# An attention and ReGLU kernel in static order: other planning figures, and 160 groups of exponentials on VectorE in place of 158

## The chip, the core and the metric

The kernel runs on one core of a Trainium2 chip. The core has five engines that each work through a queue of their own in order: TensorE (PE in the profile; PEld is its loading of weights), VectorE (DVE), ScalarE (ACT), GpSimd (POOL) and SyncE (SP), which here issues nearly all DMAs. The metric is the device time of one execution in microseconds. Several executions of one build are taken and their median is compared. Besides these, one execution is recorded by the hardware profiler; all durations below come from it.

## The reference

The input x has 2048 rows of 512. After a layer norm, two branches are added to x: attention with 32 heads of 16, and a feed-forward part with 1792 hidden units.

```
xn = layernorm(x)
q, k, v = split(xn @ wqkv)                       # 32 heads of 16
p = softmax(q k^T / 4);  A = (p v) @ wo
g = xn @ W_gate;  h = relu(g) * (xn @ W_up);  B = h @ W_down
out = x + A + B
```

Heads are so narrow that the softmax is the large part: 32 x 2048 x 2048 exponentials, 134 million.

## The kernel before

**Tiles and blocks.** The queries are cut into four chunks of 512 (c4), the heads into four groups of eight (gg), and each group is passed over twice (ee), four heads at a time. That makes 32 blocks. A block goes over 16 key tiles of 128 keys. One key tile of a block holds scores for 4 heads x 128 keys x 512 queries, that is four PSUM banks of 128 x 512.

**Two ways to take the exponential.** Usually a key tile becomes two *units* of two banks each. For a unit, TensorE writes the two banks of scores (L1461 loads k), ScalarE takes the exp of both in one instruction (L1525, 128 x 1024) into a ring of SBUF buffers, and TensorE multiplies them with v (L1433 loads v) into an accumulating bank. The score banks of ScalarE are two pairs; the next but one unit reuses a pair, so a score waits for the exp two units earlier.

For some key tiles, called *groups* here (`quad` in the code, `QUADS` by block), VectorE makes the exponential out of integers: it evicts each of the four score banks with an addition and a maximum into 16-bit integers that, read as bf16, are a stepwise power of two (L1481). GpSimd then makes two copies shifted by a constant, 64 bits at a time (`int64_add`, L1495); for the first two and the last two groups VectorE does that (L1498). All three versions are multiplied with v and add up, which smooths the steps. So a group costs four evictions, two additions and three passes with v, where a key tile on ScalarE costs two exps and one pass. Before, 158 of 512 key tiles are groups: 708 exps and 632 evictions. Where in its block a group stands follows from `QUADS` and `QOFF`; block 0 has none.

**Work beside attention.** The projections of q and k (`proj_q`, `proj_k`), the feed-forward part (`glu`, in pairs of 128 hidden units with two weight buffers, evictions L1130 and L1134) and the rows of the output (`out_rows`, L1172 and L1178, which multiply with W_down in Wd, Wk and Wv and with wo in Wo_p) are called *jobs*. They get places counted in units: projections some 32 to 48 units ahead of their use, feed-forward and rows spread evenly up to `NU - 60`, where NU is the number of units. Weights of the feed-forward part are fetched `W_LEAD` units before their job, in four pieces 6 units apart; rows of an output block come at the earliest `ROW_AT` units after the block of queries ends.

**What sets the order.** Nothing is decided on the chip. `Graph.run` simulates the engines with a fixed duration for each operation (`dur`), a hand-over time for each engine (`LAT`) and priorities, and so lists every engine's instructions; `Graph.emit` writes these lists out with the semaphore waits that they need. An exp counts 904 ns and a hand-over of 176, a GpSimd addition 1060 and 150, an eviction 601 and 135. A group's scores may be made up to `AHEAD` = 10 units before its own place. Filler matmuls are let in ahead of a score only if the plan says that the score is still in time for ScalarE (`fits`). What runs on the chip is the list, each instruction starting when its engine is free and its waits are over.

## Time and profile before

| | before |
|---|---|
| median of 3 runs | 684.08 us (683.42 to 684.76) |
| the profiled execution's own time | 682.77 us |
| its span, first to last instruction | 680.6 us |
| granted TensorE clock | 1.000 of full speed |
| first and last start of an exp | 10.3 and 668.4 us |
| DMA traffic | 28.77 MB, 42 GB/s on average |

The span is shorter than the time by the 2.17 us around it. In the groups of instructions, a row gives the line, engine, operation, the tiles written and read, the number of instructions, then the busy time in us and the mean duration of one in ns, then the idle time of the engine just ahead of them and who ended it. Instructions of one engine overlap (an exp's record is 1117 ns long while the next one starts after some 900), so a duration isn't a step. Matmul ends are modelled. The table of 20 us stretches gives, for each engine, busy us and the number of instructions.

### The profile page before, as it was taken

The numbers are of one execution on the slowest core, as the hardware profiler recorded it, in microseconds if no ns is written. First come the engines' busy times: TensorE is split into PE (matmuls) and PEld (weight loads), VectorE is DVE, ScalarE is ACT, GpSimd is POOL, SyncE is SP. The second block draws the span as 40 slices with busy tenths as digits, with TensorE's granted clock in tenths as the row PEclk, the third lists the DMA queues.
The fourth block names the chain that finished last, engine by engine and source line by source line (L and its number), as shares of the span: only waits on it lengthen the run. The fifth ranks groups of instructions, "written<-read, shape, count | busy, mean of one in ns | idle before, by whom it ended". The sixth has DMA issues, their size and how long they took to land.

```text
span 680.6 us, 46065 instructions
## 1 busy us (share of the span) xinstructions
PE 671.9 (99%) x22322; PEld 397.0 (58%) x20890; DVE 587.0 (86%) x993; ACT 659.8 (97%) x725; POOL 330.8 (49%) x341
## 2 busy tenths in 40 slices
PE   8999999999999999999999999999999999999997
PEld 3565665557565556566655656655555665655574
DVE  8957997999999878888999886889999887998876
ACT  7999999999999999999999999999999999999984
POOL 3302443564556555544556654445556654546540
PEclk9999999999999999999999999999999999999999
DMA  6520011133200121010101111110100121120001
GB/s 202 88 51 21 19 38 42 46 90 80 69 21 21 37 57 44 21 37 16 41 10 23 42 46 50 26 40 22 35 5 21 36 78 33 43 60 13 21 13 35
DMA packets 51478, 28.77 MB, mean 42 GB/s; under 512 B 18840, under 2 KB 50328, under 8 KB 51288
## 3 DMA queue, kind: packets, MB, share of 16 engines
q1 hardware_dynamic: 51144, 25.70, 14.8%
q8 instruction: 169, 2.77, 1.7%
q14 instruction: 21, 0.17, 0.1%
q10 hardware_dynamic: 144, 0.13, 0.1%
HBM read 18.22 MB, written 2.10 MB: 30 GB/s over the span
## 4 chain that ended last, share of the span: by engine, by line
PE 85%; ACT 10%; DVE 4%; issue 0%; DMA 0%; POOL 0%; DVEq 0%
PE ps L138 85%; ACT ring L1525 10%; DVE stats L810 1%; DMA x_sb<-in_A_x_dram 0%; DVE qd L1481 0%; DVE xn_sb L833 0%; DVE qd L1498 0%; DVE mv L812 0%; DVE xn_sb L1298 0%; POOL rstd L794 0%; DVE v_aug L978 0%; DVE kT L971 0%; DVE xnT L878 0%; DVE qT L1065 0%; DVE up_sb L1277 0%
## 5 line engine op out<-in xcount | busy, mean ns | idle before, releaser
L1525 ACT ACTIVATE ring<-ps 128x1024 bf16<-128x1024 f32 x708 | 651.9, 1117 | 7.3 <-PE ps L138 6.5
L1495 POOL INT64_ADD qd<-qd x308 | 317.3, 1040 | 308.9 <-DVE qd L1481 173.5
L138 PE MATMUL ps<-qT,kT 64*32 64x512 bf16 x8192 | 464.5, 375 | 1.2 <-DVE kT L971 0.4
L1481 DVE TENSOR_SCALAR qd<-ps 128x512 int16<-128x512 f32 x632 | 412.8, 684 | 59.6 <-PE ps L138 53.0
L138 PE MATMUL ps<-qd,v_aug 64*32 64x512 bf16 x3792 | 302.2, 375 | 0.2
L138 PE MATMUL ps<-ring,v_aug 64*32 64x512 bf16 x2832 | 242.4, 375 | 0.1
L1461 PEld LDWEIGHTS <-kT 64*32 64x32 bf16 x8132 | 175.3, 92 | 110.0 <-issue 24.4
L1433 PEld LDWEIGHTS <-v_aug 64*32 64x32 bf16 x5252 | 128.6, 92 | 63.9 <-issue 10.1
L138 PE MATMUL ps<-xnT,wgs 64*32 64x512 bf16 x1792 | 137.0, 375 | 0.0
L138 PE MATMUL ps<-xnT,wus 64*32 64x512 bf16 x1792 | 135.3, 375 | 0.0
L138 PE MATMUL ps<-Wd,hT 64*32 64x512 bf16 x768 | 58.6, 375 | 0.3 <-issue 0.2
L913 PEld LDWEIGHTS <-hT 64*32 64x32 bf16 x1792 | 43.9, 92 | 24.1 <-issue 3.7
L913 PEld LDWEIGHTS <-wgs 64*32 64x32 bf16 x1792 | 43.7, 92 | 22.8 <-issue 3.5
L913 PEld LDWEIGHTS <-wus 64*32 64x32 bf16 x1792 | 43.8, 92 | 22.5 <-issue 3.3
L1130 DVE COPY up_sb<-ps 128x512 f32<-128x512 f32 x56 | 38.3, 685 | 7.3 <-PE ps L138 7.3
L138 PE MATMUL ps<-Wv,hT 64*32 64x512 bf16 x512 | 40.3, 375 | 0.4 <-issue 0.4
L1134 DVE SCALAR_TENSOR_TENSOR hT<-ps,up_sb 128x512 bf16<-128x512 f32 x56 | 38.3, 683 | 2.7 <-PE ps L138 2.5
L138 PE MATMUL ps<-Wk,hT 64*32 64x512 bf16 x512 | 39.6, 375 | 0.0
L138 PE MATMUL ps<-Wo_p,x_sb 64*32 64x512 bf16 x480 | 37.7, 376 | 0.1
L138 PE MATMUL ps<-xnT,Wq 64*32 64x512 bf16 x480 | 37.1, 375 | 0.0
L138 PE MATMUL ps<-xnT,Wk 64*32 64x512 bf16 x480 | 35.9, 375 | 0.3 <-DVE xnT L878 0.3
L138 PE MATMUL ps<-Wv,xnT 64*32 64x512 bf16 x512 | 30.4, 375 | 0.3
(83 smaller groups left out, 222.3 us busy)
## 6 DMA issues: line engine op xcount, KB each, us to landing
wus<-in_B_W_up_dram SPq DMA_DIRECT2D x38, 128.0 KB, 2.4
wgs<-in_B_W_gate_dram SPq DMA_DIRECT2D x38, 128.0 KB, 2.5
xr_sb<-in_A_x_dram SPq DMA_DIRECT2D x16, 128.0 KB, 2.7
qT<-qf SPq DMA_DIRECT2D x120, 16.0 KB, 2.3
o_sb<-o_sb SPq DMA_DIRECT2D x60, 32.0 KB, 2.6
out_dram<-xn_sb SPq DMA_DIRECT2D x15, 128.0 KB, 1.9
x_sb<-in_A_x_dram SPq DMA_DIRECT2D x8, 128.0 KB, 2.7
Wd<-in_B_W_down_dram SPq DMA_DIRECT2D x6, 128.0 KB, 2.7
```

What stands on the lines that cost most here:

```text
L138: return e.add_instruction(mybir.InstMatmult(name=e.bass.get_next_instruction_name(), engine=mybir.EngineType.PE, ins=[e.lower_ap(x), e.lo ...
L810: G.op("DVE", 580, lambda e, m=m: e.bn_stats(stats[:, m, :], xs(m)), reads=[t_xm[m]], writes=[t_st], prio=pr, order=last_xn if m == 4 and ...
L913: e.ldweights(w()[rows, 32 * j:32 * j + 32], tile_position=(rows.start, 32 * j))
L1130: G.op("DVE", 603, lambda e: e.tensor_copy(up_sb[:, tup.slot, :], bank_of(tu)), reads=[tu], writes=[tup], prio=-590)
L1134: G.op("DVE", 603, lambda e: e.scalar_tensor_tensor(out=hT[:, th.slot, :], in0=bank_of(tg), scalar=0.0, in1=up_sb[:, tup.slot, :], op0=ALU ...
L1433: e.ldweights(vs(j), tile_position=(64 * half, 32 * j))
L1461: e.ldweights(ks(m), tile_position=(64 * half, 32 * m))
L1481: G.op("DVE", 601, lambda e, j=j, tx=tx: e.tensor_scalar(qd[:, tq.slot, 512 * j:512 * j + 512], ps[:, BANK[tx.slot], :], IBIAS[3], 0.0, op ...
L1495: G.op("POOL", POOL_NS, lambda e, x=x, n=n: e.int64_add(x().bitcast(I64), raw().bitcast(I64), SHIFTS[n + 1] * LANES), reads=[ti, tq, t_lib ...
L1525: exp_ops[u] = G.op("ACT", 904, lambda e, tr=tr, k0=k0: e.activation(ring[:, tr.slot, :, :], ps[:, 4 * k0:4 * k0 + 2, :], ACTF.Exp, scale= ...
```

## The change

Constants change, the planner gets faster bookkeeping, and one line of its rules is new. In the plan an exp now counts 917 ns with a hand-over of 158, a GpSimd addition 1014 ns, and a GpSimd instruction that depends on TensorE, ScalarE or VectorE can start only 110 ns later than before. The groups are 160, at other places: `QUADS` says how many by block, `QOFF` where in the block, and `QUAD_SHIFT` moves single groups by one key tile. `JOB_SHIFT` moves single jobs by some units. Feed-forward and rows are spread to `NU - 68`. The weights of the feed-forward part are fetched 34 units ahead, those of W_down 3.5 units apart, and rows come at the earliest 22 units after a chunk. The maps `release` and `known` and the counter `left` remember what was searched anew each time.

```
-D_STEP = 3
-W_LEAD = 38
+D_STEP = 3.5
+W_LEAD = 34
-ROW_AT = 20
+ROW_AT = 22
-QOFF = 0.3
+QOFF = 0.2
-JOB_SHIFT = {}
-QUAD_SHIFT = {}
+JOB_SHIFT = {2: -1, 6: -4, 9: 3, 13: 4, 14: -1, 33: -1, 34: -4, 36: 2, 41: -2, 47: 1, 49: 4, 50: 1, 51: -4, 53: -1, 59: -9, 71: 2, 72: -4, 73: -1, 75: -2, 78: -2, 79: 3, 80: -1, 83: 5, 84: -4, 88: -1, 89: -1, 92: -1, 97: 4}
+QUAD_SHIFT = {(1, 3): 1, (2, 1): -1, (4, 0): -1, (6, 0): 1, (6, 3): 1, (7, 0): 1, (7, 2): 1, (8, 1): 1, (8, 4): 1, (8, 5): 1, (9, 0): 1, (9, 3): -1, (13, 1): -1, (16, 0): -1, (16, 3): 1, (18, 4): -1, (20, 2): 1, (23, 0): -1, (25, 4): -1, (26, 2): -1, (28, 0): 1, (28, 3): -1, (29, 3): 1, (30, 0): -1, (31, 1): 1}
-POOL_NS = 1060
+POOL_NS = 1014
+PACE_END = 68
+ACT_NS = 917
-QUADS = [0, 3, 4, 5, 5, 6, 5, 5, 5, 5, 6, 5, 5, 5, 5, 6, 5, 5, 5, 6, 5, 5, 5, 5, 6, 5, 5, 5, 5, 6, 5, 5]
+QUADS = [0, 2, 5, 5, 6, 6, 4, 5, 6, 5, 5, 5, 6, 5, 5, 8, 5, 5, 4, 6, 6, 4, 6, 5, 5, 5, 5, 5, 5, 6, 5, 5]
...
-    LAT = {"PE": 212.0, "ACT": 176.0, "DVE": 135.0, "POOL": 150.0, "SP": 0.0}
+    LAT = {"PE": 212.0, "ACT": 158.0, "DVE": 135.0, "POOL": 150.0, "SP": 0.0}
     SWITCH = 107.0
+    TO_POOL = 110.0
...
-                at = max(at, d.end - (self.OWN if d.eng == o.eng == "DVE" else 0.0) if ...
+                at = max(at, (self.TO_POOL if o.eng == "POOL" and d.eng not in ("POOL", "SP") else 0.0) + d.end - (self.OWN if d.eng == o.eng == "DVE" else 0.0) if ...
...
-            at += n * max((NU - 60 - at) / max(rest, 1), 1.0)
+            at += n * max((NU - PACE_END - at) / max(rest, 1), 1.0)
...
-            exp_ops[u] = G.op("ACT", 904, lambda e, tr=tr, k0=k0: e.activation(...
+            exp_ops[u] = G.op("ACT", ACT_NS, lambda e, tr=tr, k0=k0: e.activation(...
```

More of the change, by code (lines that the diff above doesn't have):

```diff
@@ L127, in __init__ @@
         self.r = []
+        self.left = 0
 class Op:
@@ L132 @@
                  "done", "left", "users", "signal", "sem", "val", "waits", "stream", "lat", "seq", "cseq", "hb", "after", "mode", "half", "bank", "urgent", "slack", "port",
-                 "load", "wsrc", "wkey", "wwaits", "pair")
+                 "load", "wsrc", "wkey", "wwaits", "pair", "held")
 def matmul_loaded(e, out, w, x, start, stop, at):
@@ L215, in run @@
             o.users = []
+            o.held = []
+        for t in {t for o in ops for t in o.acq} | {c for o in ops for t in o.acq for c in t.pool.cur if c is not None}:
+            us = set(t.w + t.r)
+            t.left = len(us)
+            for o in us:
+                o.held.append(t)
         for o in ops:
@@ L238, in slot_for @@
                 else:
-                    us = c.w + c.r
-                    if not all(u.done for u in us):
-                        continue
-                    at = max(u.end for u in us)
+                    at = release.get(c)
+                    if at is None:
+                        if c.left:
+                            continue
+                        at = release[c] = max(u.end for u in c.w + c.r)
                 if best is None or at < best[0]:
@@ L261, in run, with bound, ready @@
         last = {}
-        def ready(o):
+        known, release = {}, {}
+        def bound(o):
             at = 0.0
             for d in o.deps:
-                at = max(at, d.end - (self.OWN if d.eng == o.eng == "DVE" else 0.0) if d.eng == "PE" or d.eng == o.eng == "DVE" else d.end + ((0.0 if d.urgent else max(self.DMA_SLACK, o.slack)) if d.eng == "SP" else o.slack))
+                at = max(at, (self.TO_POOL if o.eng == "POOL" and d.eng not in ("POOL", "SP") else 0.0) + d.end - (self.OWN if d.eng == o.eng == "DVE" else 0.0) if d.eng == "PE" or d.eng == o.eng == "DVE" else d.end + ((0.0 if d.urgent else max(self.DMA_SLACK, o.slack)) if d.eng == "SP" else o.slack))
             for d in o.order:
                 at = max(at, d.start if d.eng == o.eng else d.end)
+            return at
+        def ready(o):
+            at = known.get(o)
+            if at is None:
+                at = known[o] = bound(o)
             for t in o.acq:
@@ L403, in run @@
             o.done = True
+            for t in o.held:
+                t.left -= 1
             o.seq = len(self.queue[e])
@@ L426, in run @@
                 pe["mode"] = o.mode
-                pe["at"] = at if o.mode != "half" else min(at, max(pe["at"] + self.ISSUE, ready(o), behind.end if behind is not None else 0.0))
+                pe["at"] = at if o.mode != "half" else min(at, max(pe["at"] + self.ISSUE, bound(o), behind.end if behind is not None else 0.0))
             else:
@@ L1524, in bass_parallel_sum__mha_block__glu_gated_reglu__prompt_kernel @@
             tr = Tile("r%d" % u, P_ring)
-            exp_ops[u] = G.op("ACT", 904, lambda e, tr=tr, k0=k0: e.activation(ring[:, tr.slot, :, :], ps[:, 4 * k0:4 * k0 + 2, :], ACTF.Exp, scale=EXP_SCALE),
+            exp_ops[u] = G.op("ACT", ACT_NS, lambda e, tr=tr, k0=k0: e.activation(ring[:, tr.slot, :, :], ps[:, 4 * k0:4 * k0 + 2, :], ACTF.Exp, scale=EXP_SCALE),
                               reads=[ts], writes=[tr], prio=u - 100, order=[exp_ops[u - 1]] if u else [], name="ex%d" % u)
```

## The prediction

> **What bounds the kernel now.** I read the busy times first, then the groups of instructions, then ScalarE's own timeline, then the chain of waits, and last the table of 20 us stretches.

> ```profile
> span 680.6 us, 46065 instructions
> PE 671.9 (99%) x22322; PEld 397.0 (58%) x20890; DVE 587.0 (86%) x993; ACT 659.8 (97%) x725; POOL 330.8 (49%) x341
> L1525 ACT ACTIVATE ring<-ps 128x1024 bf16<-128x1024 f32 x708 | 651.9, 1117 | 7.3 <-PE ps L138 6.5
> L1495 POOL INT64_ADD qd<-qd x308 | 317.3, 1040 | 308.9 <-DVE qd L1481 173.5
> L1481 DVE TENSOR_SCALAR qd<-ps 128x512 int16<-128x512 f32 x632 | 412.8, 684 | 59.6 <-PE ps L138 53.0
> ```

> Two engines look full, TensorE (99%) and ScalarE (97%). The group row of the exp decides between them: 708 exps leave ScalarE idle for 7.3 us in all, 6.5 of them because a score came late. VectorE stands idle for 59.6 us ahead of its evictions, GpSimd for 308.9 us ahead of its additions, so neither sets the pace on average.

> ScalarE's timeline from 38 us on says what an exp costs when nothing is missing:

> ```profile
> 38.78 132.15 ACT L1525 ACTIVATE ring<-ps 128x1024 bf16<-128x1024 f32 x144 [0.96 <-PE ps L138]
> 171.14 44.15 ACT L1525 ACTIVATE ring<-ps 128x1024 bf16<-128x1024 f32 x48 [0.20 <-PE ps L138]
> 215.54 187.52 ACT L1525 ACTIVATE ring<-ps 128x1024 bf16<-128x1024 f32 x203 [0.25 <-PE ps L138]
> ...
> 571.95 81.73 ACT L1525 ACTIVATE ring<-ps 128x1024 bf16<-128x1024 f32 x89 [0.20 <-PE ps L138]
> 656.53 12.94 ACT L1525 ACTIVATE ring<-ps 128x1024 bf16<-128x1024 f32 x14 [2.85 <-PE ps L138]
> ```

> Each row is an unbroken run: start, length, number. Neighbours overlap, so the step from one exp to the next is (length less the last exp's own 1.12) over (number less 1): 0.911 in the run of 14, 0.916 in those of 144 and 89, 0.923 in that of 203. The one large hole is 2.85 us before 656.53. From the first exp's start (10.3) to the last one's (668.4) pass 658.1 us, or 0.931 per step; at 0.911 the 707 steps would take 644.1, so 14.0 us are lost to scores that come late: half as idle time (7.3), half as steps stretched inside the runs (6.7). The span is thus 10.3 of head, 658.1 of exps, 12.2 from the last exp's start to the end. The chain of waits gives TensorE 85% and the exp 10%:

> ```profile
> PE 85%; ACT 10%; DVE 4%; issue 0%; DMA 0%; POOL 0%; DVEq 0%
> ```

> That 85% does not make TensorE the bound: the chain steps to the instruction before on the same engine whenever no wait ended just then, and a TensorE with modelled, overlapping ends always has one. ScalarE's runs are the better witness.

> **The change, part by part.** Durations are of the profiled execution: span 680.6, time 682.77; the median of the runs is 684.08. So I add 2.17 and 1.31, together 3.48, to a span to get the predicted time.

> *Two key tiles go from ScalarE to VectorE* (158 groups to 160). Each tile took two exps, so 4 of 708 go: 4 x 0.915 = 3.66 us off the path, between 3.64 (0.911) and 3.69 (0.923). [...]

> What they add: 8 evictions of a score bank on VectorE at 412.8/632 = 0.653, 5.2 us; 4 additions on GpSimd at 1.04, 4.2 us; and on TensorE 32 matmuls, since a tile from VectorE is multiplied with v three times (24 matmuls) where one from ScalarE needs one pass (8). In the stretch from 560 to 600 us TensorE issued 1400 matmuls in 40 us, 0.0286 each, so 0.9 us. All three lie beside ScalarE's work: GpSimd's 4.2 in 308.9 us of idle time, TensorE's under 704 exps. VectorE's 5.2 lie in its 59.6 us, but not evenly, which is the first rival.

> *The groups move between blocks.* A block is one of the 32 passes over 16 key tiles. Blocks 2, 4, 8, 12, 20 and 22 get one group more, block 15 gets two (8 of its 16 tiles), and blocks 1, 6, 10, 18, 21 and 24 one fewer. A block with one more sheds 1.83 us of exps and gains 2.61 of evictions. By themselves these moves cost nothing where VectorE has room. Where the block is full of evictions they cost what spills over. If no work crossed a block's edge, the spill by the 20 us rows would be: around block 15 (by the count of exps at 328 to 347 us) the rows from 300 to 360 show VectorE busy 18.44 + 18.20 + 18.59 = 55.2 us of 60; 5.2 more makes 60.4 in a stretch that ScalarE would finish in 56.3, 4.1 late. For the six blocks with one more I take the mean of the two rows that each lies in, add 2.61 and take off the 18.17 that ScalarE would then need of 20: block 8 (18.08 and 18.88) spills 2.9, block 22 (18.66, 18.80) 3.2, block 2 (17.28, 18.30) 2.2, block 12 (17.88, 17.03) 1.9, block 4 (15.49, 18.48) 1.4, block 20 (15.69, 17.12) 0.8: 16.5 in all with block 15. The other end is nothing, since a group's scores may be made up to 10 exps (9.2 us, half a block) early. Two rows show a full VectorE that costs ScalarE nothing:

> ```profile
> 500.00:520.00 20.00, 20.00 (x660) 11.35 (x600) 19.34 (x33) 20.00 (x23) 12.28 (x12) 1.00 0.05 12
> ...
> 600.00:620.00 20.00, 20.00 (x648) 10.78 (x588) 19.78 (x35) 20.00 (x23) 10.31 (x10) 1.00 0.20 52
> ```

> The columns are length, then busy us and count of PE, PEld, DVE, ACT, POOL, and the clock. VectorE is at 97% and 99%, ScalarE at 100% with 23 exps. So I take a value near the covered end, 1.5 us, and keep 0 and 16.5.

> *The planner's figures* set only the order. The exp goes from 904 to 917, its hand-over from 176 to 158: planned step and hand-over end at 1075 instead of 1080. 904 is shorter than every run above, 917 lies inside 0.911 to 0.923. GpSimd's addition goes from 1060 to 1014, and its start is planned 110 later behind another engine; the trace shows runs of two additions in 2.05 to 2.07 us and single ones of 1.04, a step of about 1.02. An order planned with a true exp should stretch fewer steps. The unknown lies between nothing and all 6.7 us of stretch, and below nothing if more filler work is let in ahead of a score; I take a fifth, 1.4, because the runs already average 0.919 and planning at 0.917 gives 704 x 0.002.

> *Background jobs.* The gated weights are spread to end 8 units earlier (68 in place of 60), the rows of an output block start 2 units later, single jobs move by up to 9 units. In the stretch from 640 to 660 us TensorE works through the last rows (100 matmuls on the Wd tile alone) and ScalarE waits 2.85 us. With earlier jobs ahead and the third last one 4 units later, I give half of this back: 1.4 of 2.85, with 0 and 2.85 as ends. Weight loads are issued 4 units (3.7 us) later, but 34 units are 31 us and the last of the four pieces is issued 18 units behind the first, 14.6 us before use; it lands 2.5 us after issue. On SP's queue, moved loads pass stores and q copies, which land in 1.9 to 2.7 us; SP itself mostly waits for exps. I cost that at nothing; if the cover were gone it would be one landing, 2.7, at a time.

> The planner's new bookkeeping (remembered ready times and slot releases) returns the same answers as before, so it costs nothing on the chip.

> Sum: -3.66 - 1.4 - 1.4 + 1.5 = -4.96. Span 675.6, **time 679.1**.

> **The rivals.**
> - *VectorE sets the pace in the fuller blocks* (the other side). One mechanism: evictions that don't fit the block push the scores behind them in TensorE's static order, and the exp after them waits. Price 0 to 16.5; it makes the kernel slower by over 0.2% once more than 5.1 of these (3.66 saved and the 1.4 of 0.2%) stay and nothing else is won, 31%. For it: 55.2 of 60 busy where block 15 lies. Against it: the two rows above, and that ScalarE's losses now lie where VectorE is emptiest (400 to 420: 14.14 of 20 busy, and two of its waits). At half, 8.25: span 680.6 - 3.66 + 8.25 = 685.2, time 688.7. Chance 0.20.
> - *TensorE is the bound*, as 99% and the chain's 85% would have it. Then the exps saved count for nothing, and 32 more matmuls cost 0.9: span 681.5, time 685.0, no change. Against it: a TensorE at its limit would keep ScalarE waiting ahead of most exps, and the waits list ten of 708. Chance 0.11. [...]
> - *The new order loses almost no exp time*: all 6.5 us of waiting for scores go beside the four exps. Span 680.6 - 3.66 - 6.5 = 670.4, time 673.9. For it: 917 and 1014 lie nearer to the rows. Against: the head's share (1.3 us before 20 us) has nothing to do with groups. Chance 0.17 for under 677.
> - *It does not do what it says* (an order so near the old one that only the exps go): span 676.9, time 680.4; it lies inside my forecast, with a chance of 0.02 beside it.

> **How the numbers follow.** Forecast 0.50 (677 to 682), better 0.17, exps alone 0.02: faster 0.69. TensorE as bound: same 0.11. VectorE: slower 0.20. Within 0.2% (1.4 us) is about what a measurement of this kernel can't tell from no change. The range goes from 673.5, just under the rival that wins all waits, to 688.5, VectorE's half price; the part of that rival beyond it (0.10) and times below (0.07) are left out.

> **What would show it.** Right: 704 exps with a step of 0.91 to 0.92 in the runs, idle time before the exp under 7 us, the hole near the end smaller, 640 evictions at 0.65. Wrong: ScalarE idle between 300 and 360 us with VectorE full there; or runs with steps over 0.925; or a larger hole in the last 40 us.

## The result, and the profile after

| | before | after |
|---|---|---|
| median of 20 runs each | 684.50 us | 681.42 us |
| lowest and highest | 682.55 to 686.96 | 676.90 to 686.97 |
| profiled execution: time, span | 682.77, 680.6 | 683.30, 681.3 |

The ratio is 0.9957 with a 95% interval of 0.9938 to 0.9976: the change makes the kernel 0.43% (2.9 us) faster. The forecast was 679.1 us, 5.0 off; the time lies inside the range, and a little over half of the forecast gain of 5.0 came. Runs of the changed kernel lie much further apart, and its profiled execution is one of the slower ones. So the two profiles differ by +0.7 us of span where the medians differ by -3.1, and what is read from one profile is below checked with more of them.

The page of the changed kernel and its groups, in the columns of before:

```profile
span 681.3 us, 46196 instructions
PE 669.6 (98%) x22355; PEld 410.7 (60%) x20975; DVE 591.3 (87%) x1001; ACT 659.9 (97%) x721; POOL 334.6 (49%) x345
L1546 ACT ACTIVATE ring<-ps 128x1024 bf16<-128x1024 f32 x704 | 651.9, 1063 | 9.6 <-PE ps L141 8.4
L1516 POOL INT64_ADD qd<-qd x312 | 321.8, 1042 | 305.7 <-DVE qd L1502 189.2
L1502 DVE TENSOR_SCALAR qd<-ps 128x512 int16<-128x512 f32 x640 | 418.8, 684 | 52.1 <-PE ps L141 46.9
```

The work is what the change says: 704 exps, 640 evictions at 0.654 each, 312 additions. Yet ScalarE's busy time is 651.9 as before: four exps fewer, but the steps are longer (a step goes from one exp's start to the next; 660.4 us over 703 steps, 0.939 against 0.931). ScalarE's timeline of the changed kernel shows where:

```profile
169.17 56.54 ACT L1546 ACTIVATE ring<-ps 128x1024 bf16<-128x1024 f32 x61 [1.27 <-PE ps L141]
...
264.17 11.46 ACT L1546 ACTIVATE ring<-ps 128x1024 bf16<-128x1024 f32 x12 [0.54 <-PE ps L141]
275.90 16.60 ACT L1546 ACTIVATE ring<-ps 128x1024 bf16<-128x1024 f32 x18 [0.26 <-PE ps L141]
294.11 122.16 ACT L1546 ACTIVATE ring<-ps 128x1024 bf16<-128x1024 f32 x132 [1.61 <-PE ps L141]
...
604.16 67.61 ACT L1546 ACTIVATE ring<-ps 128x1024 bf16<-128x1024 f32 x73 [0.15 <-PE ps L141]
```

The hole of 2.85 us near the end is gone: the last 73 exps run unbroken. In exchange there are more holes before 300 us, the largest 1.61 and 1.27. Of the signs that the prediction named, 704 exps, 640 evictions at 0.65 and the smaller hole came; the idle time before the exps is 9.6 and not under 7, and several runs have steps over 0.925 (0.945 in the one of 12 at 264), which it had put down as a sign of being wrong. And the stretch where block 15 now has eight groups shows no loss at all; the table of 20 us stretches, columns as in the prediction:

```profile
300.00:320.00 20.00, 19.95 (x680) 12.28 (x628) 18.55 (x31) 20.00 (x23) 10.99 (x11) 1.00 0.12 31
320.00:340.00 20.00, 20.00 (x684) 12.23 (x624) 19.46 (x34) 20.00 (x23) 11.00 (x11) 1.00 0.18 45
340.00:360.00 20.00, 20.00 (x708) 12.42 (x644) 18.58 (x30) 20.00 (x23) 12.02 (x13) 1.00 0.03 6
```

ScalarE is busy for 20.00 of 20 in all three, with VectorE at 19.46 where its groups are densest.

**The hole of 1.61 us** can be followed instruction by instruction in two timelines around it (start, length, engine, line, and in brackets the idle time before). That of SyncE's queue:

```profile
282.73 6.76 SPq L982 DMA_DIRECT2D qT<-qf  x7
289.54 1.24 SPq L1405 DMA_DIRECT2D rb<-rrec  x2
```

and, on the other engines behind them:

```profile
292.09 0.72 DVE L1417 STREAM_SHUFFLE rb<-rb 128x512 f32<-128x512 f32 x1
292.70 0.67 DVE L1502 TENSOR_SCALAR qd<-ps 128x512 int16<-128x512 f32 x1
293.43 0.38 PE L141 MATMUL ps<-qT,kT 64*32 64x512 bf16 x4 [1.82 <-DVE qd L1502]
294.11 2.07 ACT L1546 ACTIVATE ring<-ps 128x1024 bf16<-128x1024 f32 x2 [1.61 <-PE ps L141]
```

SyncE issues seven copies of q, nearly 1 us each, and only then the two small DMAs into rb, whose input has been ready since 283.9 (the end of the reciprocal). VectorE reaches the shuffle that needs rb at 290.08 and stands until 292.09. Behind it in VectorE's queue is an eviction that TensorE needs for its next score, and behind that score is the exp: 2.0, 1.82 and 1.61 us. The waits list of this profile has three such waits, 3.1 us in all; that of before has none:

```profile
DVE rb L1417 <- DMA rb<-rrec: 3.1, 3, 2.0
```

**The hole of 1.27 us** is of another kind. The timeline of the same kernel at 168 us, the rows of TensorE and ScalarE that matter:

```profile
168.16 0.37 PE L141 MATMUL ps<-ring,v_aug 64*32 64x512 bf16 x1
...
168.75 0.38 PE L141 MATMUL ps<-ring,v_aug 64*32 64x512 bf16 x3 [0.21 <-issue]
...
169.17 1.02 ACT L1546 ACTIVATE ring<-ps 128x1024 bf16<-128x1024 f32 x1 [1.27 <-PE ps L141]
```

Four matmuls of one group mostly start together in the trace: a row of four is 0.38 us long, a single one 0.37. Here TensorE starts one, and the other three 0.59 us later, with no wait between them. I counted such stops in the traces (over 0.25 us between two starts on TensorE, matmuls and weight loads alike, the later one waiting for no semaphore, 0.06 taken off each, from 20 to 668 us): 11 before, 4.3 us; 26 after, 10.2 us. At each of these 37, a DMA packet of the instruction queue had landed 1.2 to 1.7 us before TensorE went on, and the next one started 1.05 to 1.7 us after, 1.15 at the median. Of that queue the page of the changed kernel says (packets, MB, share):

```profile
q8 instruction: 169, 2.77, 1.8%
```

169 packets and 2.77 MB are 16 KB a packet. The trace has 43,330 instructions on TensorE (22,355 matmuls and 20,975 loads). If the queue brings these, a packet holds 256 of them. One packet started every 3.85 us at the median, 3.2 at the fastest.

The places of the stops bear this out. Number everything that TensorE's queue holds by its start: in the 14 profiles of this case, 286 of 287 stops stand a multiple of 256 instructions apart from the others of their profile, that is, where one block of 256 ends and the next begins. At all such crossings (some 2,300 in the 14 profiles) the new block never starts sooner than 1.19 us after a packet landed. At the crossings up to 1.6 us after a landing 0.16 us pass between the two starts on average; at the later ones it is 0.017, about as much as the 0.015 between any two starts. So in a stop TensorE waits for instructions to arrive. It happens at 26 of 166 crossings of the changed kernel; why at these isn't known.

So two theories stood for the missing part of the gain: A, the wait for rb; B, TensorE's stops for instructions.

### The profile page after: what moved, and what is told of

It reads as the page before. It is cut to its first block, busy times and chain, and to the rows that moved or that the text cites. A ratio compares the mean times of both kernels' runs of the same rounds, so it can differ in the third digit from the quotient of the medians.

```text
span 681.3 us, 46196 instructions
## 1 busy us (share of the span) xinstructions
PE 669.6 (98%) x22355; PEld 410.7 (60%) x20975; DVE 591.3 (87%) x1001; ACT 659.9 (97%) x721; POOL 334.6 (49%) x345
## 3 DMA queue, kind: packets, MB, share of 16 engines
q8 instruction: 169, 2.77, 1.8%
## 4 chain that ended last, share of the span: by engine, by line
PE 94%; DVE 4%; DMA 1%; issue 1%; POOL 0%; DVEq 0%; SPq 0%
PE ps L141 94%; DVE qd L1502 1%; DVE stats L831 1%; DMA rb<-rrec 1%; DMA x_sb<-in_A_x_dram 0%; DVE xn_sb L854 0%; DVE mv L833 0%; DVE up_sb L1151 0%; DVE xnT L899 0%; PE ps L1275 0%; DVE qT L1086 0%; DVE xn_sb L1319 0%; DVE hT L1155 0%; DVE kT L992 0%; DVEq L605 0%
## 5 line engine op out<-in xcount | busy, mean ns | idle before, releaser
L1546 ACT ACTIVATE ring<-ps 128x1024 bf16<-128x1024 f32 x704 | 651.9, 1063 | 9.6 <-PE ps L141 8.4
L141 PE MATMUL ps<-qT,kT 64*32 64x512 bf16 x8192 | 473.6, 375 | 3.6 <-DVE qd L1502 1.8
L1516 POOL INT64_ADD qd<-qd x312 | 321.8, 1042 | 305.7 <-DVE qd L1502 189.2
L1502 DVE TENSOR_SCALAR qd<-ps 128x512 int16<-128x512 f32 x640 | 418.8, 684 | 52.1 <-PE ps L141 46.9
L141 PE MATMUL ps<-qd,v_aug 64*32 64x512 bf16 x3840 | 306.7, 375 | 0.5 <-issue 0.2
L141 PE MATMUL ps<-ring,v_aug 64*32 64x512 bf16 x2816 | 245.3, 375 | 0.8 <-issue 0.7
L1482 PEld LDWEIGHTS <-kT 64*32 64x32 bf16 x8164 | 182.2, 92 | 105.7 <-issue 26.1
L1454 PEld LDWEIGHTS <-v_aug 64*32 64x32 bf16 x5304 | 132.6, 92 | 58.9 <-issue 7.4
L141 PE MATMUL ps<-Wk,hT 64*32 64x512 bf16 x512 | 43.0, 375 | 0.0
L141 PE MATMUL ps<-xnT,Wq 64*32 64x512 bf16 x480 | 39.3, 375 | 0.0
L141 PE MATMUL ps<-Wv,xnT 64*32 64x512 bf16 x512 | 33.0, 375 | 0.4 <-issue 0.2
```

Of the source, the lines that this page charges most:

```text
L141: return e.add_instruction(mybir.InstMatmult(name=e.bass.get_next_instruction_name(), engine=mybir.EngineType.PE, ins=[e.lower_ap(x), e.lo ...
L1454: e.ldweights(vs(j), tile_position=(64 * half, 32 * j))
L1482: e.ldweights(ks(m), tile_position=(64 * half, 32 * m))
L1502: G.op("DVE", 601, lambda e, j=j, tx=tx: e.tensor_scalar(qd[:, tq.slot, 512 * j:512 * j + 512], ps[:, BANK[tx.slot], :], IBIAS[3], 0.0, op ...
L1516: G.op("POOL", POOL_NS, lambda e, x=x, n=n: e.int64_add(x().bitcast(I64), raw().bitcast(I64), SHIFTS[n + 1] * LANES), reads=[ti, tq, t_lib ...
L1546: exp_ops[u] = G.op("ACT", ACT_NS, lambda e, tr=tr, k0=k0: e.activation(ring[:, tr.slot, :, :], ps[:, 4 * k0:4 * k0 + 2, :], ACTF.Exp, sca ...
```

## The experiments

Each kernel was timed together with the kernel before on the same chip, and its ratio is to that. Differences between two ratios are in parts of 684 us.

**1. The changed kernel again** (`after_again`, no edit).

> The changed kernel once more, to see what in its profile comes back. In the first profile of it ScalarE lost 22.1 us to late steps (over 0.93 us each) against 16.8 before; 1.8 us of that stood behind one VectorE wait of 2.0 us for the DMA into rb, and TensorE stopped 26 times with no wait shown, 10.2 us in all, against 11 times and 4.3 us. Theory A (the DMA wait and its like cost most of the difference): the 2 us wait at the same instruction comes back in each profile, its length changes, and the time goes with it. Theory B (TensorE runs out of instructions that it fetches in pieces of 16 KB): the stops without a wait come back in like number, 20 to 30, at other places. Ratio to the kernel before 0.994 to 0.998 by both.

Measured: 0.9962 (0.9944 to 0.9980), runs from 677.67 to 684.66. The profiled execution (span 679.1) waits for rb once, for 1.7 us, at the same instruction (shuffle at 289.88, DMA issued at 287.37), and has 18 stops without a wait, 7.6 us, at partly other places. Both come back, the wait as theory A said, the stops a little fewer than the 20 to 30 of theory B, so this run doesn't part the two. Together they are 9.3 us here and 13.3 in the first profile, and the spans differ by 2.2.

**2. The DMAs into rb first** (`rb_first`).

```
         G.run()
+        q = G.queue["SP"]
+        for o in [o for o in q if o.stream[0] == "n2"]:
+            i = q.index(o)
+            while q[i - 1].name == "q2":
+                i -= 1
+            q.insert(i, q.pop(q.index(o)))
+        for i, o in enumerate(q):
+            o.seq = i
```

> The changed kernel with the small DMAs into rb issued ahead of the q copies that stand just before them in SyncE's queue; nothing else moves. By theory A (the DMA into rb, held up behind seven q copies of 0.6 to 1.0 us each, makes VectorE wait and TensorE after it) VectorE's waits for rb, 3.1 us in three places, go to under 0.3, and the time falls by 1.5 to 2.5 us against the changed kernel, ratio to before 0.992 to 0.9935. By theory B (instruction supply) the waits go as well, but the time stays within 0.7 us of the changed kernel, as other stops set the pace.

Measured: 0.9919 (0.9906 to 0.9932), runs from 676.88 to 678.69, on the chip of experiment 1: 677.57 against 680.75, 3.2 us less, and the intervals don't overlap. That is more than the 1.5 to 2.5 expected. The DMAs into rb go out at 280.62, right behind the reciprocal, no instruction waits for rb, and ScalarE's run from 249 to 331 us is unbroken:

```profile
249.01 81.55 ACT L1546 ACTIVATE ring<-ps 128x1024 bf16<-128x1024 f32 x88
```

Theory A holds for this hole. But the profile also has fewer stops (18, 6.5 us), so not all of the 3.2 us need be the wait's.

**3. The same once more, on another chip** (`rb_first_again`).

> The kernel with the DMAs into rb first, once more, as the base for the next two on the same chip. Ratio to before 0.990 to 0.9935, runs within 3 us of each other.

Measured: 0.9947 (0.9929 to 0.9965), runs from 677.26 to 682.23: outside what was expected, with no wait for rb but 25 stops of 10.3 us in the profiled execution (span 679.8). Over the two goes the edit is worth 0.7 to 3.2 us against the changed kernel; the lower figure alone isn't clear of noise, as the interval of this go overlaps those of the changed kernel. It is the fastest version that leaves no work out: 0.8% and 0.5% under the kernel before.

**4. The same edit on the kernel before** (`before_rb_first`).

> Control: the kernel before with the same move in SyncE's queue, the DMAs into rb ahead of the q copies just before them. There VectorE's instruction that needs rb never waited (the profile lists no wait of it), although five of these DMAs stood behind q copies too. Theory A (only a landing that is later than VectorE's place for it costs time): nothing to win, ratio 0.999 to 1.001. Rival (earlier DMAs into rb help in general, or the copies for q are what counts): 0.995 or less, or over 1.003 if later q copies hurt.

Measured: 1.0003 (0.9993 to 1.0012). Five of its DMAs moved past q copies too and nothing came of it: in that order rb landed in time anyway. So an early DMA is worth nothing in itself there; what costs in the new order is a landing behind VectorE's place for it.

**5. More instructions on TensorE** (`rb_first_reload`).

```
             elif held[o.half] == o.wkey:
-                o.load, o.wsrc = False, ()
+                o.wsrc = ()
```

> The changed kernel with the DMAs into rb first, and every group of four matmuls loads its weights again even where they are still loaded: 1380 more weight loads on TensorE (20860 to 22240), 3% more instructions, no other order. Theory B (TensorE's instructions come in pieces of 16 KB, one in 3.9 us on average and one in 3.3 at the fastest, so its supply is nearly used up): 5 more pieces, stops without a wait rise from 18 and 6.5 us to over 30 and 10, time up by 2 to 8 us against the kernel with the DMAs first. Rival (the stops are noise and loads are hidden under matmuls): within 0.7 us.

Measured: 0.9986 (0.9967 to 1.0004), runs from 677.39 to 686.04; against the two goes without the extra loads 2.7 and 4.6 us slower, in the range that theory B gave. The instruction queue has 175 packets in place of 169. The profiled execution happens to be its fastest: 24 stops, 8.2 us, short of the 30 and 10 expected, so the rise in stops wasn't seen. A third explanation, that the extra loads take TensorE's time of their own, isn't ruled out: even the lowest run, at 0.9936 of the kernel before on its chip, lies above the lowest of the two goes without them (0.9911 and 0.9902).

**6. Less DMA traffic beside it** (`rb_first_reload_light`).

```
-    dst[:, tw.slot, dt:dt + 2, :], src[...].rearrange("(dt p) f -> p dt f", p=128)), 128,
+    dst[0:pn, tw.slot, dt:dt + 2, :], src[...].rearrange("(dt p) f -> p dt f", p=128)[0:pn]), 128,   # pn=128 if k < NWS else 8
```

> The kernel with the DMAs first and with all weight loads repeated (which gave 0.9986), but the feed-forward weights from the third buffer on are fetched for 8 of 128 partitions only: same instructions and same number of DMAs, the output leaves these weights out. Theory B in its stronger form (a piece of instructions is late because it shares the DMA engines with the weight traffic): the median time that a piece takes falls from 1.03 towards 0.9, stops without a wait fall below 10, and the time comes back to within 1 us of the kernel with the DMAs first, ratio 0.991 to 0.994. Rival (the supply's own cycle is what limits, traffic matters little): ratio 0.997 to 1.000 as with full traffic.

Measured: 1.0042 (1.0024 to 1.0060), slower, with 42 stops and 17.2 us of them; the median time of a packet was 1.09 us, against 1.03 in experiment 5. The stronger form of theory B, that weight traffic makes the packets late, falls. Why stops rose with less traffic stays open.

**7. The parts of the change alone.** Planning figures on the kernel before (`figures_only`):

> The kernel before (158 groups at the old places, old job places) with the new planning figures alone: exp 917 and 158, addition 1014, 110 more to start on GpSimd. My step in the prediction: 1.4 us off, ratio 0.998, stretched steps fewer. Rival: an order planned at 917 lets more filler in ahead of a score, steps stretch, ratio 1.000 to 1.006 with more late steps than 109. If the mean step in blocks 1 to 13 rises from 0.92 towards 0.945 as in the changed kernel, the figures carry the loss.

Measured: 1.0103 (1.0087 to 1.0120). That is more than either alternative gave. Late steps (over 0.933 us) rise from 109 to 135, 26 stops take 9.1 us, and ScalarE waits 6.4 us for TensorE after the last exp, where it waited 1.7 before. New groups on the kernel before (`groups_only`: QUADS, QOFF, QUAD_SHIFT):

> The kernel before with the 160 groups at their new places alone (figures and jobs as before): 704 exps. My sum: 3.66 off, 1.5 for VectorE on top, ratio 0.997. Rival (VectorE full in the fuller blocks): ScalarE idle around block 15 and in blocks 8 and 22, ratio over 1.004. If places and jobs fit only together, late steps rise in blocks all over and the ratio lies near 1.000.

Measured: 1.0225 (1.0207 to 1.0243), with 704 exps and 23.1 us of idle time before them. Its ScalarE timeline in parts:

```profile
508.87 29.44 ACT L1525 ACTIVATE ring<-ps 128x1024 bf16<-128x1024 f32 x32 [3.77 <-PE ps L138]
...
662.89 9.27 ACT L1525 ACTIVATE ring<-ps 128x1024 bf16<-128x1024 f32 x10 [2.54 <-PE ps L138]
```

and its 20 us stretches there:

```profile
500.00:520.00 20.00, 20.00 (x676) 12.02 (x636) 17.71 (x29) 16.23 (x19) 10.30 (x10) 1.00 0.02 5
...
660.00:680.00 20.00, 20.00 (x676) 11.06 (x628) 11.90 (x19) 14.94 (x17) 7.20 (x7) 1.00 0.05 11
```

Around block 15 it loses little. The holes stand in block 23 (VectorE 17.71 of 20 busy) and in the last two blocks (11.90): not where VectorE is fullest, but where the order has put other matmuls ahead of the scores. The list itself has these holes: `Graph.run` of this kernel plans ScalarE idle for 23.9 us between exps, 5.3 of them in block 23 and 7.5 in the last two, and the trace shows 23.1, 4.9 and 7.6. Changed kernel with the old figures (`old_figures`):

> The changed kernel (groups and jobs at their new places) with the old planning figures: exp 904 and 176, addition 1060, nothing added for GpSimd's start. My prediction's step says +1.4 us against the changed kernel, ratio to before 0.998. As the figures alone on the kernel before gave 1.0103 and the groups alone 1.0225, the theory now is that places and figures fit only as a set: 1.005 to 1.02. If the ratio stays under 0.999, the new places do the work and the figures matter little.

Measured: 1.0097 (1.0083 to 1.0111). Changed kernel with the old 158 groups (`after_158`):

> The changed kernel (new figures, jobs at their new places) with the old 158 groups: 708 exps. By my sum +3.66 us for four exps less 1.5 for VectorE, ratio 0.999. By the theory of the set: 1.005 to 1.02, with the loss spread over blocks as idle time or late steps, not as an even 0.0055 for four exps.

Measured: 1.0025 (1.0017 to 1.0034), a little under the expected 1.005, with 5 stops of 1.3 us only and 111 late steps.

| figures | groups | jobs | ratio |
|---|---|---|---|
| old | old | old | 1 |
| new | old | old | 1.0103 |
| old | new | old | 1.0225 |
| old | new | new | 1.0097 |
| new | old | new | 1.0025 |
| new | new | new | 0.9957, 0.9962 |

The figures or the groups, put in alone or taken out of the set, are slower than before. They are no terms of a sum. The moved jobs were never timed alone, nor the set without them.

**8. Shorter exps** (`short_exps`).

```
-lambda e, tr=tr, k0=k0: e.activation(ring[:, tr.slot, :, :], ps[:, 4 * k0:4 * k0 + 2, :], ...
+lambda e, tr=tr, k0=k0, n=1 if u >= 32 and u % 16 == 0 else 2: e.activation(ring[:, tr.slot, :n, :], ps[:, 4 * k0:4 * k0 + n, :], ...
```

> The kernel with the DMAs first, in which 42 of the 704 exps (every 16th from the 32nd on) take only one of their two banks, 512 columns in place of 1024; half of those scores is left out. Nothing else changes. A copy of 512 columns on ScalarE takes 0.60 and the shortest exp of 1024 took 1.02, so 0.42 each, 17.6 us in all. If ScalarE is the bound, as the prediction has it, all of it comes off: 16 to 18 us, ratio 0.965 to 0.969. If TensorE is near its own limit behind it, much less: 5 to 12 us, ratio 0.974 to 0.985. If TensorE were the bound: under 2 us.

Measured: 0.9941 (0.9924 to 0.9958), beside 0.9947 (0.9929 to 0.9965) without the edit on the same chip: no gain that the runs can tell. The exp's row of experiment 3, then the two rows by shape of this run:

```profile
L1546 ACT ACTIVATE ring<-ps 128x1024 bf16<-128x1024 f32 x704 | 652.6, 1059 | 7.4 <-PE ps L141 6.3
...
L1546 ACT ACTIVATE ring<-ps 128x1024 bf16<-128x1024 f32 x662 | 621.8, 1037 | 19.1 <-PE ps L141 15.2
L1546 ACT ACTIVATE ring<-ps 128x512 bf16<-128x512 f32 x42 | 26.3, 627 | 0.1
```

ScalarE is busy for some 10 us less in all (650.6 against 660.6) and idle ahead of its exps for 11.7 more (19.1 against 7.4, of which 15.2 and 6.3 are put down to late scores): the time that it was given turned into waiting for TensorE. The profile is of the slowest of its 12 runs, with 35 stops of 13.5 us beside 25 of 10.3 in experiment 3; these 3.2 us are a small part of 17.6. In this order ScalarE isn't what sets the pace. The order of the kernel before was not tested so.

**9. Shorter matmuls** (`short_matmuls`).

```
+                    pvn[0] += 1
+                    nc = 128 if pvn[0] % 11 == 3 and 0 < st[0] < st[1] - 1 else 512
                     for j in range(4):
-                        ins = matmul_loaded(e, ps[..., BANK[t.slot], :], vs(j), src[j](rows), ...
+                        ins = matmul_loaded(e, ps[..., BANK[t.slot], 0:nc], vs(j), src[j](rows)[:, 0:nc], ...
```

> The kernel with the DMAs into rb first (ratio 0.9919 and 0.9947 in two goes), in which 568 of the 22354 matmuls, spread evenly over the passes with v, take 128 columns in place of 512; the rest of these products is left out. Same instructions, same order, same exps. In the trace half the array starts a group of four matmuls every 0.2145 us, so a short group saves 0.16 of its half, and 142 groups save 142 x 0.16 / 2 = 11.4 us of TensorE. Shortening 42 exps by 17.6 us in all had given nothing. If TensorE's array time sets the pace through the whole kernel: 8 to 12 us off, ratio 0.975 to 0.982. If the supply of instructions does (their number is unchanged): under 3 us, ratio 0.990 or more, and more stops without a wait. If ScalarE does after all: under 2 us. If the static order holds all engines to one beat, so that relief of one engine alone is worth little: 2 to 6 us.

Measured: 0.9896 (0.9880 to 0.9911), 1.6 and 3.5 us under the two goes without the edit, which ran on other chips: 14% to 31% of the estimated 11.4 us. The records of the short matmuls are 0.215 us long on average, those of the full ones 0.375 (ends are modelled): the 0.16 less that the expectation took. The interval overlaps that of experiment 2 (0.9906 to 0.9932), so the lower figure alone isn't clear of noise. TensorE's array time alone isn't the bound through the whole kernel either. The chain of waits of experiment 2, then the chain and the exp's row of this run show what takes over:

```profile
PE 96%; DVE 2%; DMA 0%; issue 0%; ACT 0%; SPq 0%; POOL 0%; DVEq 0%
...
PE 79%; ACT 16%; DVE 3%; issue 1%; DMA 0%; POOL 0%; DVEq 0%
...
L1548 ACT ACTIVATE ring<-ps 128x1024 bf16<-128x1024 f32 x704 | 649.8, 1094 | 4.5 <-PE ps L141 3.3
```

With TensorE relieved, ScalarE comes into the chain, and it stands idle for only 4.5 us. Stops didn't rise (20, 7.2 us). So the last alternative of the expectation fits best, a static order that ties the engines to one beat: relief of ScalarE is worth nothing, relief of TensorE a few us until ScalarE is next.

The profiles of the changed order side by side, the last two rows with work left out, show what goes with the time:

| profile | stops without a wait | wait for rb | span |
|---|---|---|---|
| rb_first | 18, 6.5 us | 0 | 675.1 |
| rb_first_reload | 24, 8.2 us | 0 | 675.5 |
| after_again | 18, 7.6 us | 1.7 | 679.1 |
| rb_first_again | 25, 10.3 us | 0 | 679.8 |
| changed kernel, first | 26, 10.2 us | 3.1 | 681.3 |
| rb_first_reload_light | 42, 17.2 us | 0 | 684.4 |
| short_exps | 35, 13.5 us | 0 | 681.9 |
| short_matmuls | 20, 7.2 us | 0 | 674.1 |

The two goes of `rb_first` are the same program: 3.8 us more of stops, 4.7 us more of span.

## Why the prediction was right and where it failed

The direction and the range were right, the size only roughly; the reason given for the size was not. That the sum came within 2.3 us is partly luck: none of its four terms came as priced, and the wait for rb and TensorE's stops, which it put at nothing or didn't foresee, took back several us.

- *"Two engines look full ... ScalarE's runs are the better witness"*, so four exps are 3.66 us off the path: this is the step that failed, as far as the changed order shows it. Experiment 8 took an estimated 17.6 us of exps away from the same order and the time stayed. Runs of exps at 0.911 to 0.923 a step show that ScalarE mostly runs at its own speed, but not that its time alone is worth anything: the next score came no sooner, and ScalarE stood idle for 11.7 us more. In experiment 9 relief of TensorE by an estimated 11.4 us brought 1.6 to 3.5 and put ScalarE into the chain. The prediction took one engine for the bound where two were tied. It also measured the loss against too long a step: its rule gives 0.909 for the run of 14, not 0.911, and half of the 707 steps in the trace of before are 0.904 or less, so some 19 us were lost to late scores there, not 14.0.
- *The rival "TensorE is the bound"* (0.11, no change) fails by the result, and by experiment 9 as far as it means TensorE's array time alone. Its first half, that the exps saved count for nothing, is what experiment 8 shows. ScalarE's 97% of busy time was no bound that could be relieved alone (0.9941 against 0.9947).
- *VectorE in the fuller blocks*, 1.5 us taken of 0 to 16.5: near the covered end as it said, and even less. ScalarE was busy for 60.00 of 60 us from 300 to 360. The rival (0.20) did not come.
- *The planner's figures*, 1.4 us off as a term of its own: wrong in kind. Alone they cost 1.03%, and taken out of the set they cost 1.4% (1.0097 against 0.9957). Nor is 917 the true exp: the median step before is 0.904, the old figure. And the 110 ns ahead of GpSimd, told of in the change and the prediction, do not act: as the line is written, its condition lets them in only where the instruction waited for is one of TensorE, and no GpSimd instruction has such a wait when it is planned. With `TO_POOL` at 0 `Graph.run` makes the same five lists.
- *Background jobs*, half of the 2.85 us hole: mis-sized, as all of it went. That the jobs did it isn't shown: with the new figures alone the largest hole in the last 40 us of exps is already only 0.48, though ScalarE then waits 6.4 us after them.
- *"On SP's queue, moved loads pass stores and q copies ... I cost that at nothing; if the cover were gone it would be one landing, 2.7, at a time"*: the cover was gone, at one place above all. It was not a moved weight load that came late, as the step had in mind: DMAs into rb stood behind q copies, and VectorE waited 2.0 and 1.7 us in two profiles. Putting them first won 0.7 to 3.2 us. The price named was about right; the step failed in taking it as hidden.
- Not foreseen at all: stops of TensorE without a wait, 4.3 us before and 7.6 and 10.2 after. They, and the wait for rb, are what the runs show of the missing 2 us. They are also the likely reason why its runs scatter over 10 us where those of before lie within 4.4: the two profiles of `rb_first` differ by 3.8 us of stops and 4.7 of span.

That TensorE waits for its instructions in these stops is shown by their places, at crossings of 256 instructions and 1.2 to 1.7 us behind a packet's landing. That they make up the difference in time is supported by the table but not shown: experiment 5 leaves another explanation, the attempt to make packets faster brought more of them, and what decides how many there are stays open.

## What to carry to other kernels

A busy engine with few holes was not yet a bound in this statically ordered kernel (ScalarE busy for 660.6 of 679.8 us with 7.4 us of holes in experiment 3, and 17.6 us of exps less, by estimate, brought no gain that the runs can tell): shorten its work in place and see whether the time follows, before pricing an edit by that engine's durations. Planning figures and places found together were worth something only together here, so a diff of them can't be summed part by part. Look through SyncE's queue at each place where a burst of copies was moved: here two small DMAs behind seven copies (6.76 us of issues) held VectorE for 2.0 us, and TensorE for 1.82 and ScalarE for 1.61 behind it.
